# Linear attention's denominators as 32 rows per 512 tokens on four column tiles, with the reciprocals spread to the partitions by DMA

## The chip, the cores and the metric

One Trainium2 chip, one of its cores. The metric is the device time of one execution in microseconds (us). The kernel before takes 504.74 us (median of 4 runs, 504.45 to 505.67).

Names of engines: PE multiplies matrices, PEld loads its weights, DVE is the vector engine, ACT the scalar (activation) engine, POOL the general-purpose engine, SP the one that issues most DMAs. PSUM is the memory that PE writes (8 banks of 512 floats per partition).

## The reference

Two attention blocks over the same `x` (2048 tokens, width 1024, 32 heads of 32) are mixed by a gate per token. Block A is linear attention, block B a local dilated attention that this change does not touch.

```python
x = A_x
g = sigmoid((x * gate_w).sum(-1, keepdims=True))
# block A, linear attention
q, k, v = split(x @ wqkv)                      # 32 heads of 32
phi = lambda t: where(t > 0, t + 1, exp(t)) + 1e-6
pq, pk = phi(q), phi(k)
kv  = einsum("bhsd,bhse->bhde", pk, v)         # 32 x 32 per head
z   = einsum("bhsd->bhd", pk)                  # 32 per head
num = einsum("bhqd,bhde->bhqe", pq, kv)
den = einsum("bhqd,bhd->bhq", pq, z)[..., None] + 1e-6
a   = merge_heads(num / den) @ A_wo
# block B: 8 keys per query, 2 apart, softmax, then @ B_wo     (not touched)
return g * a + (1 - g) * b
```

## The kernel before

The program lists its operations, with an estimated cost for each, and a planner orders them once, when the kernel is built. After that each engine is given its own list, in a fixed order, and waits on semaphores where an operand is not there yet. For a DMA the planner assumes that it lands `lat` us after the previous one, plus 2 us.

```python
            fin = o.end
            if o.chan is not None:
                dma_free = max(dma_free, o.end) + o.lat
                fin = dma_free + 2.0
```

In the last third of the kernel ("stage 3") `phi(q)` is made per chunk `u` of 512 tokens and per group `j` of four heads (128 partitions). `num / den` is got by scaling `phi(q)` with `1/den` first; `kv` has been folded into the output weights. `zbd` is a block-diagonal 128x128 matrix per group which holds each `z` 32 times, so that one full matmul gives each denominator already repeated on the 32 partitions that need it.

```python
        def numer(u, j):
            ...                                    # 8 matmuls of 512 columns into a bank
            phi(bank, p_, preg, 8 * u + j)         # ACT Exp, two DVE operations
            def over():
                db = main.next()
                P.op("pe", lambda e: e.matmul(db.ap(), zbd[:, j, :], p_, start=True, stop=True), ...)
                R, _ = RAr.next()
                P.op("act", ... activation(R, db.ap(), ACT.Ln, bias=eps) ...)
                P.op("act", ... activation(R, R, ACT.Exp, scale=-1.0) ...)
                P.op("dve", ... tensor_tensor(dst, p_, R, ALU.mult) ...)
            after(6 if u == 0 else 2, over)

        for n, (u, j) in enumerate(nums):          # 32 numerator groups
            numer(u, j)
            slot(0)
            if n == 1:
                turn()
            if 3 <= n < 11:
                fold(n - 3, 0); fold(n - 3, 1)
            if n >= 17:
                a_out(*outs.pop(0))                # output groups of A: 8 matmuls each, 128 tokens x 512 columns
                slot(0)
        ...                                        # rest of a_out, then 16 final tiles with B's output
```

Of the kernel before, what the change touches and what calls it, by code (L numbers as in the profile page):

```python
# [6 lines left out]
ACT = mybir.ActivationFunctionType  # L7
ALU = mybir.AluOpType
# [7 lines left out]
DH = 32  # L16
# [1086 lines left out]
def build_kernel(nc, A_x, A_wqkv, A_wo, B_x, B_wqkv, B_wo, gate_w, out):  # L1103
# [10 lines left out]
    def SB(shape, dtype, name, at=None):  # L1114
        n = SZ[dtype]
        for d in shape[1:]:
            n *= d
        if at is None:
            at = base[0]
            base[0] += (n + 31) // 32 * 32  # L1120
        uid[0] += 1
        h = nc.alloc_sbuf_tensor_at("%s_%d" % (name, uid[0]), list(shape), dtype, offset=at)
        return Tile("S", h, at, list(shape), dtype)
# [32 lines left out]
    GT = [("M", 1, 2, None)]  # L1156
    gt_hbm = nc.dram_tensor("gt_hbm", [4, 512], F32)

    def hb(p0, p1, half):
# [19 lines left out]
    kvbd = SB([128, 8, 128], BF16, "kvbd")  # L1179
    zbd = SB([128, 8, 128], BF16, "zbd")  # L1180
    kva = SB([128, 8, 33], F32, "kva")
# [16 lines left out]
    kvT = SB([128, 8, 128], BF16, "kvT", at=vr.t[1].lo)  # L1198
    RAr = Ring([SB([128, 512], F32, "ra%d" % i, at=t.lo) for i, t in enumerate((Er.t[0], Er.t[1], Lr.t[0], vr.t[0]))])
    mxr = SB([1, 4, 128], F32, "mxr", at=vr.t[2].lo)  # L1200
# [7 lines left out]
    osb = Ring([SB([128, 1024], BF16, "o%d" % i) for i in range(2)])  # L1208
    pr = Ring([SB([128, 512], BF16, "p%d" % i) for i in range(4)])
    base[0] = max(base[0], top_)  # L1210
# [12 lines left out]
    def plan(seen):  # L1223
# [45 lines left out]
        C("pool", lambda e: e.memset(kvbd[:], 0.0), 0.9, [kvbd.all()])  # L1269
        C("pool", lambda e: e.memset(zbd[:], 0.0), 0.9, [zbd.all()])  # L1270

# [288 lines left out]
        for j in range(4):  # L1560
            sl = slice(32 * j, 32 * j + 32)
            P.op("dve", lambda e, sl=sl: e.tensor_copy(zbd[sl, :, sl], kva[sl, :, 32:33].to_broadcast([32, 8, 32])), dps(256), reads=[kva.all()], writes=[zbd.all()])
            P.op("dve", lambda e, sl=sl: e.tensor_copy(kvbd[sl, :, sl], kva[sl, :, 0:32]), 0.3, reads=[kva.all()], writes=[kvbd.all()])
# [23 lines left out]
        def numer(u, j):  # L1587
            bank = main.next()
            w, wr = w_cols(2, j)
            xs, xr = x_chunk(u)  # L1590
            group(bank, w, xs, [wr, xr])
            tgt, c0 = pqn(u)
            dst, reg = tgt[:, j, c0:c0 + 512], tgt.part((j, j + 1), (c0, c0 + 512))
            if u == 0:
                p_, preg = dst, reg
            else:
                pt, _ = pr.next()
                p_, preg = pt[:, :], pt.all()
            phi(bank, p_, preg, 8 * u + j)
            def over():  # L1600
                db = main.next()
                P.op("pe", lambda e: e.matmul(db.ap(), zbd[:, j, :], p_, start=True, stop=True), mm(512), reads=[zbd.all(), preg], writes=[db.iv], name="den")  # L1602
                R, _ = RAr.next()
                P.op("act", lambda e: e.activation(R[:, :], db.ap(), ACT.Ln, bias=eps[:, :]), act(512), reads=[db.iv, eps.all()], writes=[R.all()])  # L1604
                P.op("act", lambda e: e.activation(R[:, :], R[:, :], ACT.Exp, scale=-1.0), act(512), reads=[R.all()], writes=[R.all()])  # L1605
                P.op("dve", lambda e: e.tensor_tensor(dst, p_, R[:, :], ALU.mult), 0.65, reads=[preg, R.all()], writes=[reg])
            after(6 if u == 0 else 2, over)

# [19 lines left out]

        nums = [(u, j) for u in range(4) for j in range(8)]
        outs = [(t, jh) for t in range(NT) for jh in range(2)]  # L1630
        for n, (u, j) in enumerate(nums):
            numer(u, j)
            slot(0)
            if n == 1:
                turn()
            if 3 <= n < 11:
                fold(n - 3, 0)
                fold(n - 3, 1)
            if n >= 17:
                a_out(*outs.pop(0))  # L1640
                slot(0)
        while later:
            slot(0)
        P.op("dve", lambda e: e.tensor_reduce(mx4[:, 2:3], qe[:, :], AX.X, ALU.max), 0.2, reads=[qe.all()], writes=[mx4.part((2, 3))], prio=1e5)
        while outs:
            a_out(*outs.pop(0))


        P.op("dve", lambda e: e.tensor_scalar(mx4[:, 1:2], mx4[:, 1:2], -1.0, None, op0=ALU.mult), 0.1, reads=[mx4.part((1, 2))], writes=[mx4.part((1, 2))], prio=1e5)

        def mx_out(e):
            with nc.allow_non_contiguous_dma(reason="512 maxima"):
                return e.dma_start(mx_hbm.rearrange("i p -> p i"), mx4[:, :])
        P.op("sp", mx_out, 0.6, reads=[mx4.all()], writes=[MX], chan="mxo", lat=8.0, prio=1e5)
        P.op("sp", lambda e: e.dma_start(mxr[0:1, :, :], mx_hbm[None, :, :]), 0.1, reads=[MX], writes=[mxr.all()], chan="mxi", lat=2.0, prio=1e5)
        P.op("dve", lambda e: e.tensor_reduce(mx1[:, :], mxr[:, :, :], AX.X, ALU.max), dps(512), reads=[mxr.all()], writes=[mx1.all()], prio=1e5)
        small = [mx1.all()]
        P.op("dve", lambda e: e.tensor_scalar(mx1[:, 2:3], mx1[:, 2:3], 2.0, None, op0=ALU.max), 0.1, reads=small, writes=small, prio=1e5)
        for o, i0, i1 in ((ALU.max, 0, 1), (ALU.mult, 0, 0), (ALU.mult, 2, 3)):
            P.op("dve", lambda e, o=o, i0=i0, i1=i1: e.tensor_tensor(mx1[:, i0:i0 + 1], mx1[:, i0:i0 + 1], mx1[:, i1:i1 + 1], o), 0.1, reads=small, writes=small, prio=1e5)  # L1660
        P.op("dve", lambda e: e.tensor_scalar(mx1[:, 0:1], mx1[:, 0:1], 40.0 / DH, None, op0=ALU.is_le), 0.1, reads=small, writes=small, prio=1e5)
        P.op("dve", lambda e: e.tensor_scalar(mx1[:, 2:3], mx1[:, 2:3], 1e18 / (4 * DH), None, op0=ALU.is_le), 0.1, reads=small, writes=small, prio=1e5)
        flag_op = P.op("dve", lambda e: e.tensor_tensor(flag[:, :], mx1[:, 0:1], mx1[:, 2:3], ALU.mult), 0.1, reads=small, writes=[flag.all()], prio=1e5)


        for t in range(NT):
            tgt, c0 = a_loc(t)
# [3 lines left out]
            for f0, f1 in parts:  # L1671
# [13 lines left out]
                if t == NT - 1 or f1 == 1024:  # L1685
                    c = f0 if t == NT - 1 else 0
                    P.op("sp", lambda e, e_=e_, r=r, o_=o_, c=c, f1=f1: e.dma_start(out2[e_, r * 128:(r + 1) * 128, c:f1], o_[:, c:f1]), 0.5,
                         reads=[o_.part((c, f1))], chan="out%d_%d" % (os_, c), lat=1.0)

        C("act", lambda e: e.preload_act_table_set("natural_log_exp_and_others"), 1.3, [])  # L1690
# [64 lines left out]
```

## Time and profile before

| | before |
|---|---|
| time, median of 4 (range) | 504.74 us (504.45 to 505.67) |
| span of the profiled execution | 502.5 us |
| stage 3 (explained below), first to last matmul | 170.0 us |
| last matmul's start to the end of the span | 4.6 us |

From the profile's page: the busy time of each engine (us, share of the span, instructions), and the chain of work that ended last, by engine.

```profile
PE 488.5 (97%) x5190; PEld 232.6 (46%) x5257; DVE 264.6 (53%) x456; ACT 192.9 (38%) x335; POOL 6.6 (1%) x30
...
PE 95%; issue 2%; DMA 1%; ACT 1%; SPq 0%; DVE 0%
```

PE is the limit, and the chain confirms it: what happens elsewhere costs only where PE waits.

The windows view of the stretch that changes: length, then busy us (and instructions) of PE, PEld, DVE, ACT and POOL, the granted clock, the DMA engines' busy share, and GB/s.

```profile
342.00:362.00 20.00, 19.82 (x90) 8.73 (x91) 16.33 (x31) 18.07 (x41) 0.00 (x0) 1.00 0.00 1
362.00:382.00 20.00, 19.89 (x93) 9.09 (x93) 14.67 (x27) 12.33 (x26) 0.00 (x0) 1.00 0.00 1
382.00:402.00 20.00, 19.89 (x93) 9.02 (x94) 12.21 (x22) 10.98 (x24) 0.00 (x0) 1.00 0.00 1
```

PE has next to no gaps, and the DMA engines are all but idle. The waits of PE there, 322 to 445 us (engine, waited for: us in total, times, longest):

```profile
PE ps_all L1324 <- issue: 0.2, 1, 0.2
```

The groups that the change replaces (busy us, mean ns of one, idle before it and why):

```profile
L1602 PE MATMUL ps_all<-p,zbd 128*128 128x512 bf16 x24 | 8.9, 380 | 0.0
L1602 PE MATMUL ps_all<-pq,zbd 128*128 128x512 bf16 x8 | 3.0, 379 | 0.0
L1604 ACT ACTIVATE ra<-ps_all,eps 128x512 f32<-128x512 f32 x32 | 21.5, 688 | 2.2 <-PE ps_all L1602 2.0
L1605 ACT ACTIVATE ra<-ra 128x512 f32<-128x512 f32 x32 | 19.9, 639 | 0.5
```

A matmul's 379 ns is its latency; one starts every 0.216 us. So the 32 denominators cost 32 x 0.216 = 6.9 us of PE. The DMA issue table (count, KB each, us from issue to landing): the first line below, a store of four rows, has no landing time, because the trace has 5 semaphore updates from DMA for it, where all others but one have 16.

```profile
gt_hbm<-gts SPq DMA_DIRECT2D x1, 8.0 KB
gt<-gt_hbm SPq DMA_DIRECT2D x1, 8.0 KB, 4.8
```

### The profile page before, as it was taken

The numbers are of one execution on the slowest core, as the hardware profiler recorded it, in microseconds if no ns is written. First come the engines' busy times: TensorE is split into PE (matmuls) and PEld (weight loads), VectorE is DVE, ScalarE is ACT, GpSimd is POOL, SyncE is SP. The second block draws the span as 40 slices with busy tenths as digits, with TensorE's granted clock in tenths as the row PEclk, the third lists the DMA queues.
The fourth block names the chain that finished last, engine by engine and source line by source line (L and its number), as shares of the span: only waits on it lengthen the run. The fifth ranks groups of instructions, "written<-read, shape, count | busy, mean of one in ns | idle before, by whom it ended". The sixth has DMA issues, their size and how long they took to land.

```text
span 502.5 us, 11582 instructions
## 1 busy us (share of the span) xinstructions
PE 488.5 (97%) x5190; PEld 232.6 (46%) x5257; DVE 264.6 (53%) x456; ACT 192.9 (38%) x335; POOL 6.6 (1%) x30
## 2 busy tenths in 40 slices
PE   8999999999999999999999999999999999999996
PEld 2444444444454444544544545444444444444443
DVE  3112235556667676454555464678776563234443
ACT  1111111111354454655554555479864543100000
POOL 5000000000000000000000000000000000000000
PEclk9999999999999999999999999999999999999999
DMA  8999990000024060100010100500000000011222
GB/s 222 207 204 314 353 270 1 1 0 1 12 86 139 22 198 27 34 23 23 23 39 21 33 1 3 170 0 1 0 2 0 2 0 1 1 43 64 83 78 73
DMA packets 47410, 34.92 MB, mean 69 GB/s; under 512 B 22261, under 2 KB 43125, under 8 KB 47354
## 3 DMA queue, kind: packets, MB, share of 16 engines
q1 hardware_dynamic: 46810, 33.59, 23.6%
q8 instruction: 43, 0.70, 0.6%
q10 hardware_dynamic: 544, 0.52, 0.4%
q14 instruction: 13, 0.11, 0.1%
HBM read 21.51 MB, written 8.40 MB: 60 GB/s over the span
## 4 chain that ended last, share of the span: by engine, by line
PE 95%; issue 2%; DMA 1%; ACT 1%; SPq 0%; DVE 0%
PE ps_all L1324 76%; PE ps_all L1677 11%; PE ps_all L1427 2%; PE ps_all L1447 2%; PE ps_all L1602 1%; PE ps_all L1452 1%; PE ps_all L1523 1%; DMA xT<-in_A_x_dram 1%; PE ps_all L1580 1%; ACT ra L1604 0%; PE ps_all L1392 0%; SPq L1294 0%; SPq L1299 0%; ACT e L1333 0%; ACT ra L1605 0%
## 5 line engine op out<-in xcount | busy, mean ns | idle before, releaser
L1324 PE MATMUL ps_all<-w,xT 128*128 128x512 bf16 x922 | 207.8, 379 | 5.6 <-issue 4.0
L1324 PE MATMUL ps_all<-xT,w 128*128 128x512 bf16 x747 | 169.2, 379 | 2.5 <-issue 1.9
L1324 PEld LDWEIGHTS ps_all<-w,xT 128*128 128x128 bf16 x960 | 91.3, 98 | 110.3 <-issue 1.7
L1324 PEld LDWEIGHTS ps_all<-xT,w 128*128 128x128 bf16 x768 | 73.9, 98 | 88.8 <-ACT ra L1604 0.6
L1677 PE MATMUL ps_all<-w,qT 128*128 128x512 bf16 (+1 forms) x259 | 55.2, 373 | 0.3
L1677 PEld LDWEIGHTS ps_all<-w,qT 128*128 128x128 bf16 x264 | 25.8, 98 | 29.7
L1335 DVE TENSOR_SCALAR e<-e 128x512 bf16<-128x512 bf16 x64 | 18.4, 291 | 38.9 <-ACT e L1331 25.3
L1355 DVE CAST vst<-ps_all 128x512 bf16<-128x512 f32 x15 | 10.4, 691 | 42.7 <-PE ps_all L1324 42.7
L1433 ACT ACTIVATE E<-ps_all 128x1824 bf16<-128x1824 f32 (+1 forms) x18 | 30.4, 1687 | 3.1 <-PE ps_all L1427 2.0
L1331 ACT ACTIVATE e<-ps_all 128x512 bf16<-128x512 f32 x32 | 19.1, 597 | 31.6 <-PE ps_all L1324 30.8
L1333 ACT ACTIVATE e<-ps_all 128x512 bf16<-128x512 f32 x32 | 19.2, 601 | 29.3 <-PE ps_all L1324 27.8
L1681 DVE SCALAR_TENSOR_TENSOR o<-ps_all,gm,xT 128x512 bf16<-128x512 f32 (+1 forms) x25 | 18.2, 729 | 23.0 <-PE ps_all L1677 22.8
L1280 DVE TENSOR_TENSOR mx<-mx,kT 128x1024 bf16<-128x1024 bf16 x32 | 20.7, 688 | 16.9 <-ACT kT L1356 16.8
L1280 DVE TENSOR_TENSOR mx<-mx,qT 128x1024 bf16<-128x1024 bf16 x32 | 20.7, 688 | 16.7 <-ACT qT L1359 16.6
L1356 ACT ACTIVATE vst<-ps_all 128x512 bf16<-128x512 f32 x17 | 10.1, 597 | 47.8 <-PE ps_all L1324 47.8
L1436 DVE TENSOR_TENSOR E<-E,msk 128x1824 bf16<-128x1824 bf16 (+1 forms) x18 | 19.8, 1100 | 14.5 <-ACT E L1433 14.5
L1462 DVE TENSOR_TENSOR qT<-ps_all,L 128x456 bf16<-128x456 f32 (+1 forms) x36 | 21.1, 624 | 7.7 <-ACT L L1461 7.7
L1359 ACT ACTIVATE qT<-ps_all 128x512 bf16<-128x512 f32 x15 | 9.0, 597 | 37.0 <-PE ps_all L1324 37.0
L1337 DVE SCALAR_TENSOR_TENSOR pk<-ps_all,e 128x512 bf16<-128x512 f32 x32 | 22.0, 688 | 0.8
L1604 ACT ACTIVATE ra<-ps_all,eps 128x512 f32<-128x512 f32 x32 | 21.5, 688 | 2.2 <-PE ps_all L1602 2.0
L1356 ACT ACTIVATE az<-ps_all 128x512 bf16<-128x512 f32 x19 | 11.4, 600 | 27.6 <-PE ps_all L1324 27.6
L1356 ACT ACTIVATE kT<-ps_all 128x512 bf16<-128x512 f32 x14 | 8.4, 597 | 35.5 <-PE ps_all L1324 35.5
(77 smaller groups left out, 336.5 us busy)
## 6 DMA issues: line engine op xcount, KB each, us to landing
w<-in_A_wqkv_dram SPq DMA_DIRECT2D x6, 1024.0 KB, 8.2
v<-vB_hbm SPq DMA_DIRECT2D x36, 128.0 KB, 2.6
vB_hbm<-vst SPq DMA_DIRECT2D x32, 128.0 KB, 4.9
w<-in_B_wqkv_dram SPq DMA_DIRECT2D x4, 1024.0 KB, 8.3
out_dram<-o SPq DMA_DIRECT2D x15, 256.0 KB, 2.0
w<-in_A_wo_dram SPq DMA_DIRECT2D x2, 1024.0 KB, 5.6
w<-in_B_wo_dram SPq DMA_DIRECT2D x2, 1024.0 KB, 6.5
w<-in_B_wqkv_dram SPq DMA_DIRECT2D x6, 256.0 KB, 4.1
```

What stands on the lines that cost most here:

```text
L1280: P.op("dve", lambda e, m=m, op=op: e.tensor_tensor(m[:, 0:n], m[:, 0:n], src, op), 0.08 + n / 1920.0, reads=[m.all(), reg], writes=[m.all()],
L1324: last = e.matmul(bank.ap(), lhs(dc), rhs(dc), start=(dc == 0), stop=(dc == 7))
L1331: P.op("act", lambda e: e.activation(e_[:, :], bank.ap(), ACT.Exp), act(512), reads=[bank.iv], writes=[e_.all()])
L1333: P.op("act", lambda e: e.activation(e_[:, :], bank.ap(), ACT.Exp, accum_out=qe[:, col:col + 1]), act(512) + 0.1, reads=[bank.iv], writes= ...
L1335: P.op("dve", lambda e: e.tensor_scalar(e_[:, :], e_[:, :], 1.0, 1e-6, op0=ALU.min, op1=ALU.add), 0.25, reads=[e_.all()], writes=[e_.all()])
L1337: P.op("dve", lambda e: e.scalar_tensor_tensor(out=dst, in0=bank.ap(), scalar=0.0, in1=e_[:, :], op0=ALU.max, op1=ALU.add), dps(512), read ...
L1356: fa = lambda e: e.activation(dst, src(), ACT.Copy)
L1433: P.op("act", lambda e: e.activation(E[:, 0:32 * nq].rearrange("p (j q) -> p j q", j=4), ps[:, 4:8, 0:8 * nq], ACT.Exp), act(32 * nq), rea ...
L1436: P.op("dve", lambda e: e.tensor_tensor(ev(), ev(), m[:, :, :].rearrange("p r q -> p (r q)")[:, None, :].to_broadcast([128, 16, 2 * nq]), ...
L1462: P.op("dve", lambda e, L=L, pb=pb, g=g: e.tensor_tensor(qT[:, 4 * g:4 * g + 4, t0 + qs:t0 + qs + 2 * nq].rearrange("p c (h q) -> p h c q" ...
L1604: P.op("act", lambda e: e.activation(R[:, :], db.ap(), ACT.Ln, bias=eps[:, :]), act(512), reads=[db.iv, eps.all()], writes=[R.all()])
L1677: last = e.matmul(bank.ap(0, f1 - f0), qT[:, dc, t * 128:(t + 1) * 128], ws[3][:, dc, f0:f1], start=(dc == 0), stop=(dc == 7))
```

## The change

The intent: stop spending a full 128-column matmul on each group of four heads only to repeat every denominator 32 times. With `zsel`, 32 columns per group, eight groups fit into one PSUM bank on four column tiles that work side by side: 8 narrow matmuls per chunk in place of 8 full ones, and one Ln and one Exp per chunk in place of eight. The repetition moves to DMA: the tile of reciprocals is written to DRAM and read back eight times, each read spreading four rows over 128 partitions. To give this way time, the output groups start three numerator groups later, and three output tiles are moved ahead of the last chunk's output groups.

```diff
-    zbd = SB([128, 8, 128], BF16, "zbd")
+    zsel = SB([128, 8, 32], BF16, "zsel")
+    rc_hbm = nc.dram_tensor("rc_hbm", [4, 128, 512], F32)
+    RBr = Ring([SB([128, 512], F32, "rb%d" % i, at=kT.lo + 2048 * i) for i in range(12)])
...
+        def over(u):
+            tgt, c0 = pqn(u)
+            db = main.next()
+            def fn(e):
+                for q in range(2):
+                    for c in range(4):
+                        last = e.matmul(db.ap()[32 * c:32 * c + 32, :], zsel[:, 2 * c + q, :], tgt[:, 2 * c + q, c0:c0 + 512], start=(q == 0), stop=(q == 1),
+                                        tile_position=(0, 32 * c), skip_group_check=True)
+                return last
+            P.op("pe", fn, 0.55, mode="c", ...)
+            ...                                   # ACT: Ln, then Exp(-x), on R [128, 512]
+            P.op("sp", lambda e: e.dma_start(rc_hbm[u, :, :], R[:, :]), 0.5, ..., lat=1.0)
+            for j in range(8):
+                B, bs = RBr.next()
+                r0 = 32 * (j // 2) + 4 * (j % 2)
+                src = rc_hbm[u, r0:r0 + 4, :][:, None, :].to_broadcast([4, 32, 512])
+                last_in[0] = P.op("sp", lambda e, B=B, src=src: e.dma_start(B[:, :], src), 0.5, ..., chan="rci%d" % bs, lat=1.2)
+                P.op("dve", lambda e, B=B, dst=dst: e.tensor_tensor(dst, dst, B[:, :], ALU.mult), 0.65, ...)
...
+            if j == 7:
+                after(3, lambda u=u: over(u))     # denominators of chunk u: three groups after its last numerators
-            if n >= 17:
+            if n >= 20:
                 a_out(*outs.pop(0))
...
+        EARLY = 3
+        for t in range(EARLY):
+            while len(outs) > 8:
+                a_out(*outs.pop(0))
+            final(t)
```

More of the change, by code (lines that the diff above doesn't have):

```diff
@@ L1198, in build_kernel @@
     kvT = SB([128, 8, 128], BF16, "kvT", at=vr.t[1].lo)
-    RAr = Ring([SB([128, 512], F32, "ra%d" % i, at=t.lo) for i, t in enumerate((Er.t[0], Er.t[1], Lr.t[0], vr.t[0]))])
+    RAr = Ring([SB([128, 512], F32, "ra%d" % i, at=t.lo) for i, t in enumerate((Er.t[0], Er.t[1]))])
+    RBr = Ring([SB([128, 512], F32, "rb%d" % i, at=kT.lo + 2048 * i) for i in range(12)])
     mxr = SB([1, 4, 128], F32, "mxr", at=vr.t[2].lo)
@@ L1208, in build_kernel @@
     osb = Ring([SB([128, 1024], BF16, "o%d" % i) for i in range(2)])
-    pr = Ring([SB([128, 512], BF16, "p%d" % i) for i in range(4)])
     base[0] = max(base[0], top_)
@@ L1269, in plan @@
         C("pool", lambda e: e.memset(kvbd[:], 0.0), 0.9, [kvbd.all()])
-        C("pool", lambda e: e.memset(zbd[:], 0.0), 0.9, [zbd.all()])
+        C("pool", lambda e: e.memset(zsel[:], 0.0), 0.3, [zsel.all()])
         C("dve", lambda e: e.memset(warm[:, :], 0.0), 0.15, [warm.all()])
@@ L1561, in plan @@
             sl = slice(32 * j, 32 * j + 32)
-            P.op("dve", lambda e, sl=sl: e.tensor_copy(zbd[sl, :, sl], kva[sl, :, 32:33].to_broadcast([32, 8, 32])), dps(256), reads=[kva.all()], writes=[zbd.all()])
+            for b in range(2):
+                P.op("dve", lambda e, sl=sl, b=b, c=4 * b + j: e.tensor_copy(zsel[sl, b:8:2, c:c + 1], kva[sl, b:8:2, 32:33]), 0.1, reads=[kva.all()], writes=[zsel.all()])
             P.op("dve", lambda e, sl=sl: e.tensor_copy(kvbd[sl, :, sl], kva[sl, :, 0:32]), 0.3, reads=[kva.all()], writes=[kvbd.all()])
@@ L1592, in numer @@
             tgt, c0 = pqn(u)
-            dst, reg = tgt[:, j, c0:c0 + 512], tgt.part((j, j + 1), (c0, c0 + 512))
-            if u == 0:
-                p_, preg = dst, reg
-            else:
-                pt, _ = pr.next()
-                p_, preg = pt[:, :], pt.all()
-            phi(bank, p_, preg, 8 * u + j)
-            def over():
-                db = main.next()
-                P.op("pe", lambda e: e.matmul(db.ap(), zbd[:, j, :], p_, start=True, stop=True), mm(512), reads=[zbd.all(), preg], writes=[db.iv], name="den")
-                R, _ = RAr.next()
-                P.op("act", lambda e: e.activation(R[:, :], db.ap(), ACT.Ln, bias=eps[:, :]), act(512), reads=[db.iv, eps.all()], writes=[R.all()])
-                P.op("act", lambda e: e.activation(R[:, :], R[:, :], ACT.Exp, scale=-1.0), act(512), reads=[R.all()], writes=[R.all()])
-                P.op("dve", lambda e: e.tensor_tensor(dst, p_, R[:, :], ALU.mult), 0.65, reads=[preg, R.all()], writes=[reg])
@@ L1607, in numer @@
-            after(6 if u == 0 else 2, over)
+            phi(bank, tgt[:, j, c0:c0 + 512], tgt.part((j, j + 1), (c0, c0 + 512)), 8 * u + j)
+        last_in = [None]
+        def over(u):
[7 more added lines that the diff above has]
+                return last
+            P.op("pe", fn, 0.55, mode="c", reads=[zsel.all(), tgt.part((0, 8), (c0, c0 + 512))], writes=[db.iv], name="den")
+            R, rs = RAr.next()
+            RC = [("R", u, u + 1, None)]
+            P.op("act", lambda e: e.activation(R[:, :], db.ap(), ACT.Ln, bias=eps[:, :]), act(512), reads=[db.iv, eps.all()], writes=[R.all()])
+            P.op("act", lambda e: e.activation(R[:, :], R[:, :], ACT.Exp, scale=-1.0), act(512), reads=[R.all()], writes=[R.all()])
+            P.op("sp", lambda e: e.dma_start(rc_hbm[u, :, :], R[:, :]), 0.5, reads=[R.all()], writes=[RC], chan="rco%d" % rs, lat=1.0)
+            for j in range(8):
+                B, bs = RBr.next()
+                r0 = 32 * (j // 2) + 4 * (j % 2)
+                src = rc_hbm[u, r0:r0 + 4, :][:, None, :].to_broadcast([4, 32, 512])
+                last_in[0] = P.op("sp", lambda e, B=B, src=src: e.dma_start(B[:, :], src), 0.5, reads=[RC], writes=[B.all()], chan="rci%d" % bs, lat=1.2)
+                dst, reg = tgt[:, j, c0:c0 + 512], tgt.part((j, j + 1), (c0, c0 + 512))
+                P.op("dve", lambda e, B=B, dst=dst: e.tensor_tensor(dst, dst, B[:, :], ALU.mult), 0.65, reads=[reg, B.all()], writes=[reg])
@@ L1627, in a_out @@
                 move(dst, src, 512, hold[h], reg, g[:, t:t + 1], [g.all()])
-        nums = [(u, j) for u in range(4) for j in range(8)]
-        outs = [(t, jh) for t in range(NT) for jh in range(2)]
-        for n, (u, j) in enumerate(nums):
-            numer(u, j)
-            slot(0)
-            if n == 1:
-                turn()
-            if 3 <= n < 11:
-                fold(n - 3, 0)
-                fold(n - 3, 1)
-            if n >= 17:
-                a_out(*outs.pop(0))
-                slot(0)
@@ L1642, in plan @@
-        while later:
-            slot(0)
-        P.op("dve", lambda e: e.tensor_reduce(mx4[:, 2:3], qe[:, :], AX.X, ALU.max), 0.2, reads=[qe.all()], writes=[mx4.part((2, 3))], prio=1e5)
-        while outs:
-            a_out(*outs.pop(0))
-        P.op("dve", lambda e: e.tensor_scalar(mx4[:, 1:2], mx4[:, 1:2], -1.0, None, op0=ALU.mult), 0.1, reads=[mx4.part((1, 2))], writes=[mx4.part((1, 2))], prio=1e5)
-        def mx_out(e):
-            with nc.allow_non_contiguous_dma(reason="512 maxima"):
-                return e.dma_start(mx_hbm.rearrange("i p -> p i"), mx4[:, :])
@@ L1654, in plan @@
-        P.op("sp", mx_out, 0.6, reads=[mx4.all()], writes=[MX], chan="mxo", lat=8.0, prio=1e5)
-        P.op("sp", lambda e: e.dma_start(mxr[0:1, :, :], mx_hbm[None, :, :]), 0.1, reads=[MX], writes=[mxr.all()], chan="mxi", lat=2.0, prio=1e5)
-        P.op("dve", lambda e: e.tensor_reduce(mx1[:, :], mxr[:, :, :], AX.X, ALU.max), dps(512), reads=[mxr.all()], writes=[mx1.all()], prio=1e5)
-        small = [mx1.all()]
-        P.op("dve", lambda e: e.tensor_scalar(mx1[:, 2:3], mx1[:, 2:3], 2.0, None, op0=ALU.max), 0.1, reads=small, writes=small, prio=1e5)
@@ L1659, in plan @@
-        for o, i0, i1 in ((ALU.max, 0, 1), (ALU.mult, 0, 0), (ALU.mult, 2, 3)):
-            P.op("dve", lambda e, o=o, i0=i0, i1=i1: e.tensor_tensor(mx1[:, i0:i0 + 1], mx1[:, i0:i0 + 1], mx1[:, i1:i1 + 1], o), 0.1, reads=small, writes=small, prio=1e5)
-        P.op("dve", lambda e: e.tensor_scalar(mx1[:, 0:1], mx1[:, 0:1], 40.0 / DH, None, op0=ALU.is_le), 0.1, reads=small, writes=small, prio=1e5)
-        P.op("dve", lambda e: e.tensor_scalar(mx1[:, 2:3], mx1[:, 2:3], 1e18 / (4 * DH), None, op0=ALU.is_le), 0.1, reads=small, writes=small, prio=1e5)
@@ L1663, in plan, with final @@
-        flag_op = P.op("dve", lambda e: e.tensor_tensor(flag[:, :], mx1[:, 0:1], mx1[:, 2:3], ALU.mult), 0.1, reads=small, writes=[flag.all()], prio=1e5)
-        for t in range(NT):
+        def final(t):
             tgt, c0 = a_loc(t)
@@ L1688, in plan @@
                          reads=[o_.part((c, f1))], chan="out%d_%d" % (os_, c), lat=1.0)
+        nums = [(u, j) for u in range(4) for j in range(8)]
+        outs = [(t, jh) for t in range(NT) for jh in range(2)]
+        for n, (u, j) in enumerate(nums):
+            numer(u, j)
+            if j == 7:
+                after(3, lambda u=u: over(u))
+            slot(0)
+            if n == 1:
+                turn()
+            if 3 <= n < 11:
+                fold(n - 3, 0)
+                fold(n - 3, 1)
+            if n >= 20:
+                a_out(*outs.pop(0))
+                slot(0)
@@ new lines, in plan @@
+        while later:
+            slot(0)
+        P.op("dve", lambda e: e.tensor_reduce(mx4[:, 2:3], qe[:, :], AX.X, ALU.max), 0.2, reads=[qe.all()], writes=[mx4.part((2, 3))], prio=1e5)
+        EARLY = 3
+        for t in range(EARLY):
+            while len(outs) > 8:
+                a_out(*outs.pop(0))
+            final(t)
+        while outs:
+            a_out(*outs.pop(0))
+        P.op("dve", lambda e: e.tensor_scalar(mx4[:, 1:2], mx4[:, 1:2], -1.0, None, op0=ALU.mult), 0.1, reads=[mx4.part((1, 2))], writes=[mx4.part((1, 2))], prio=1e5)
@@ new lines, in mx_out @@
+        def mx_out(e):
+            with nc.allow_non_contiguous_dma(reason="512 maxima"):
+                return e.dma_start(mx_hbm.rearrange("i p -> p i"), mx4[:, :])
+        P.op("sp", mx_out, 0.6, reads=[mx4.all()], writes=[MX], chan="mxo", lat=8.0, prio=1e5, after=[last_in[0]])
+        P.op("sp", lambda e: e.dma_start(mxr[0:1, :, :], mx_hbm[None, :, :]), 0.1, reads=[MX], writes=[mxr.all()], chan="mxi", lat=2.0, prio=1e5)
+        P.op("dve", lambda e: e.tensor_reduce(mx1[:, :], mxr[:, :, :], AX.X, ALU.max), dps(512), reads=[mxr.all()], writes=[mx1.all()], prio=1e5)
@@ new lines, in plan @@
+        small = [mx1.all()]
+        P.op("dve", lambda e: e.tensor_scalar(mx1[:, 2:3], mx1[:, 2:3], 2.0, None, op0=ALU.max), 0.1, reads=small, writes=small, prio=1e5)
+        for o, i0, i1 in ((ALU.max, 0, 1), (ALU.mult, 0, 0), (ALU.mult, 2, 3)):
+            P.op("dve", lambda e, o=o, i0=i0, i1=i1: e.tensor_tensor(mx1[:, i0:i0 + 1], mx1[:, i0:i0 + 1], mx1[:, i1:i1 + 1], o), 0.1, reads=small, writes=small, prio=1e5)
+        P.op("dve", lambda e: e.tensor_scalar(mx1[:, 0:1], mx1[:, 0:1], 40.0 / DH, None, op0=ALU.is_le), 0.1, reads=small, writes=small, prio=1e5)
@@ L1690, in plan @@
+        P.op("dve", lambda e: e.tensor_scalar(mx1[:, 2:3], mx1[:, 2:3], 1e18 / (4 * DH), None, op0=ALU.is_le), 0.1, reads=small, writes=small, prio=1e5)
+        flag_op = P.op("dve", lambda e: e.tensor_tensor(flag[:, :], mx1[:, 0:1], mx1[:, 2:3], ALU.mult), 0.1, reads=small, writes=[flag.all()], prio=1e5)
+        for t in range(EARLY, NT):
+            final(t)
         C("act", lambda e: e.preload_act_table_set("natural_log_exp_and_others"), 1.3, [])
```

## The prediction

> # Prediction
>
> **What bounds the kernel.** PE. The page's busy table: PE 488.5 of 502.5 us (97%), DVE 53%, ACT 38%. The chain of waits is 95% PE. In the stretch that changes (322 to 443 us, windows view) PE is busy 19.8 to 19.9 of every 20 us; the waits of PE there sum to 0.2 us. A 512-column matmul costs 0.216 us of PE (10.79 us per 50 in the chain). DMA is idle from 330 to 440 us.
>
> **Removed.** 32 full-array denominator matmuls: 32 x 0.216 = 6.9 us of PE, all on the chain. Also 28 of 32 Ln and Exp pairs (0.69 + 0.64 us), 37 us of ACT, off the chain.
>
> **Added on PE.** Four groups of 8 matmuls on 4 column tiles. The gate has this shape: 32 matmuls in 1.84 us, so four run together, 0.23 us a round. Two rounds plus the mode change (issue gaps of 0.16 us beside the score groups; the Trainium skill, TensorEngine Tiling (Array Packing), Key Properties, says a mode change drains the engine) is about 0.55 us, 2.2 us in all. PE gains 4.5 to 5 us: 500 us if nothing waits.
>
> **Added on DMA, and why I doubt 500.** Per 512 tokens, one 256 KB write and eight 256 KB broadcast reads whose source has an outermost size of 4. The Trainium skill, DMA: Bandwidth & Descriptors, "Why a DMA increments its semaphore by 16 and not by 1", says the engines used are the largest number up to 16 that divides both outermost sizes: 4 here. This trace agrees for the 4-row gate store: 5 semaphore updates came from DMA where others have 16, and the issue table has no landing time for it. A 2 KB packet took a median 84 to 87 ns, so a chunk's 1024 packets over 4 engines take about 21.5 us (estimate); over 16, 5.4 us. The kernel's planner assumes 9.6 us.
>
> Denominator to last scaled tile (estimate): 0.5 PE, 1.35 Ln and Exp, 2.5 write, 2 first read, 21.5 reads, 0.7 multiply, 1 of semaphores: 29.5 us. Between the first chunk's denominators and the first output group reading it, PE has 11 numerator groups (1.73 each), 4 folds, one denominator group: 20.4 us. PE waits about 9 us there. For later chunks enough PE work lies between (31 us for the last, with the 3 moved tiles), but DVE runs in an order planned for earlier landings: its multiplies come 8 to 10 us late and hold PSUM evacuations behind them. Eight banks cover some 8 us, so about 3 us more over three chunks.
>
> **Sum.** 504.9 - 4.7 + 9 + 3 = 512; the moved tiles look tuned on a chip, so I shade it to 510. Range 499.5 to 518. Faster by over 2%: 2%; within: 78%; slower: 20%.
>
> **What would show it.** PE busy falls to about 484 us. The reads have no landing time; DMA share is near a quarter for 20 us per chunk. PE waits for DVE's multiply 6 to 11 us once near 350 to 365 us; DVE waits for reads 2.7 us apart. If 16 engines serve the reads, the share is near 1 for 6 us, nothing waits, and the time is 500. The end is unchanged.
>
> **What would make it wrong.** Reads spread over 16 engines; packets faster than 84 ns; the planner putting other PE work before the first output group; deeper DVE blocking than eight banks cover, which costs 10 us more.

## The result

| | before | after |
|---|---|---|
| time, median of 4 (range) | 504.74 us (504.45 to 505.67) | 518.86 us (517.12 to 519.31) |
| ratio | | 1.0273 (95%: 1.0254 to 1.0292) |
| span of the profiled execution | 502.5 us | 517.6 us |
| stage 3, first to last matmul, same matmuls | 171.7 us | 182.9 us |
| last matmul's start to the end of the span | 4.6 us | 6.9 us |

The stage row is read from the trace: from the transposes of `turn()` to the last matmul. The kernel after has one numerator group more in that stretch (8 weight loads more), so 8 x 0.216 = 1.7 us are added to the 170.0 us of before.

The change makes the kernel 2.7% slower, just outside the range (499.5 to 518) that I gave. The same views of the kernel after, first the page: busy times, then two rows of 40 slices of the span (granted clock in tenths; DMA busy share in tenths), and the chain.

```profile
PE 498.6 (96%) x5257; PEld 231.6 (45%) x5257; DVE 258.2 (50%) x452; ACT 166.8 (32%) x287; POOL 6.0 (1%) x30
...
PEclk9999999999999999999999999999797999999999
DMA  8999980000042160100100004002222212221121
...
PE 83%; DMA 10%; SPq 3%; DVE 1%; ACT 1%; issue 0%
```

In what follows L1325 is a numerator group or an output group (8 matmuls of 512 columns), L1606 the denominators, L1336 and L1338 the two DVE steps of `phi`, L1621 the multiply by the reciprocals (before: L1324, L1602, L1335, L1337, L1606).

DMA is now on the chain, and there are two slices in which PE got less than its full clock. The windows, as before:

```profile
342.00:362.00 20.00, 18.16 (x90) 7.77 (x87) 10.79 (x22) 8.43 (x23) 0.00 (x0) 1.00 0.21 79
362.00:382.00 20.00, 17.25 (x74) 7.03 (x75) 10.97 (x20) 5.62 (x14) 0.00 (x0) 0.83 0.26 101
382.00:402.00 20.00, 14.80 (x62) 5.75 (x60) 9.53 (x19) 4.59 (x11) 0.00 (x0) 0.83 0.26 98
```

DVE and ACT do less than before, so neither is short of time; PE lost matmuls (62 in 20 us where it did 93). The DMA engines sit at a quarter of their capacity, 0.26 and about 100 GB/s, for as long as the reads last: 0.26 of 16 engines is 4.2 engines' worth, the flat level to be expected if each read runs on 4 (s16, below, tests that). The new groups, and the reads in the issue table, with no landing time:

```profile
L1606 PE MATMUL ps_all<-xT,zsel 128*32 128x512 bf16 x24 | 2.7, 542 | 9.2 <-DVE xT L1338 9.2
L1612 ACT ACTIVATE ra<-ps_all,eps 128x512 f32<-128x512 f32 x4 | 2.7, 686 | 9.9 <-PE ps_all L1606 9.9
L1613 ACT ACTIVATE ra<-ra 128x512 f32<-128x512 f32 x4 | 2.5, 632 | 0.1
```

```profile
rb<-rc_hbm SPq DMA_DIRECT2D x32, 256.0 KB
```

The waits of PE, and those of DVE for the reads:

```profile
PE ps_all L1606 <- DVE xT L1338: 9.2, 2, 5.2
...
PE ps_all L1325 <- DVE pq L1621: 0.6, 1, 0.6
PE ps_all L1325 <- DVE xT L1359: 0.4, 1, 0.4
```

```profile
DVE xT L1621 <- DMA rb<-rc_hbm: 29.8, 20, 1.9
...
DVE pq L1621 <- DMA rb<-rc_hbm: 9.7, 7, 1.9
```

So PE's long waits are not where I had put them (L1325 waiting for the multiply L1621: only 0.6 us) but before the denominators of the second and the third chunk (L1606), and what they wait for is no multiply: L1338 is the last step of `phi`, which needs no reciprocal at all. The timeline of PE there (start, length, what, and the idle time before it):

```profile
364.14 1.05 PE L1606 MATMUL ps_all<-xT,zsel 128*32 128x512 bf16 x8 [3.98 <-DVE xT L1338]
365.12 5.53 PE L1325 MATMUL ps_all<-xT,w 128*128 128x512 bf16 x16
371.26 1.90 PE L1325 MATMUL ps_all<-w,pq 128*128 128x512 bf16 x8 [0.60 <-DVE pq L1621]
...
390.45 1.04 PE L1606 MATMUL ps_all<-xT,zsel 128*32 128x512 bf16 x8 [5.20 <-DVE xT L1338]
391.42 3.60 PE L1325 MATMUL ps_all<-w,pq 128*128 128x512 bf16 x8
```

and of DVE just before the first of these waits ended:

```profile
357.68 0.69 DVE L1621 TENSOR_TENSOR pq<-pq,rb 128x512 bf16<-128x512 bf16 x1 [0.95 <-DMA rb<-rc_hbm]
360.25 0.69 DVE L1621 TENSOR_TENSOR pq<-pq,rb 128x512 bf16<-128x512 bf16 x1 [1.88 <-DMA rb<-rc_hbm]
360.85 0.49 DVE L1336 TENSOR_SCALAR e<-e 128x512 bf16<-128x512 bf16 x2
362.80 0.69 DVE L1621 TENSOR_TENSOR pq<-pq,rb 128x512 bf16<-128x512 bf16 x1 [1.45 <-DMA rb<-rc_hbm]
363.40 0.68 DVE L1338 SCALAR_TENSOR_TENSOR xT<-ps_all,e 128x512 bf16<-128x512 f32 x1
```

Read it from below: `phi`'s last step (363.40) stands behind the multiply at 362.80 in DVE's fixed list, which waits for a read; the reads land 2.56 us apart. The multiply does not concern the second chunk, but DVE cannot pass it. PE, which needs that `phi` for the second chunk's denominators, idles until 364.14. And after each wait PE runs slow: 16 matmuls take 5.53 us, where they take 3.63 at full clock (junk, below). The trace's clock records show half clock from 362.18 to 369.01 and from 389.49 to 396.32, 6.83 us each.

### The profile page after: what moved, and what is told of

Same layout as the page of the kernel before. It is cut to its first block, busy times and chain, and to the rows that moved or that the text cites. A ratio compares the mean times of both kernels' runs of the same rounds, so it can differ in the third digit from the quotient of the medians. Undisturbed runs are those within 1.5% of the kernel's fastest.

```text
span 517.6 us, 11655 instructions
## 1 busy us (share of the span) xinstructions
PE 498.6 (96%) x5257; PEld 231.6 (45%) x5257; DVE 258.2 (50%) x452; ACT 166.8 (32%) x287; POOL 6.0 (1%) x30
## 4 chain that ended last, share of the span: by engine, by line
PE 83%; DMA 10%; SPq 3%; DVE 1%; ACT 1%; issue 0%
PE ps_all L1325 65%; PE ps_all L1654 11%; DMA rb<-rc_hbm 8%; SPq L1619 3%; PE ps_all L1428 2%; PE ps_all L1448 2%; DMA rc_hbm<-ra 2%; PE ps_all L1453 1%; DMA xT<-in_A_x_dram 1%; PE ps_all L1524 1%; PE ps_all L1606 1%; PE ps_all L1582 1%; ACT ra L1612 0%; DVE xT L1338 0%; PE ps_all L1393 0%; ACT ra L1613 0%
## 5 line engine op out<-in xcount | busy, mean ns | idle before, releaser
L1325 PE MATMUL ps_all<-w,xT 128*128 128x512 bf16 x960 | 215.7, 382 | 1.3 <-DMA xT<-in_A_x_dram 0.9
L1325 PE MATMUL ps_all<-xT,w 128*128 128x512 bf16 x768 | 174.3, 383 | 0.0
L1325 PEld LDWEIGHTS ps_all<-w,xT 128*128 128x128 bf16 x960 | 91.9, 98 | 112.1 <-issue 5.2
L1325 PEld LDWEIGHTS ps_all<-xT,w 128*128 128x128 bf16 x768 | 74.7, 99 | 91.4 <-issue 5.3
L1336 DVE TENSOR_SCALAR e<-e 128x512 bf16<-128x512 bf16 x64 | 18.4, 290 | 33.1 <-ACT e L1332 25.2
L1356 DVE CAST vst<-ps_all 128x512 bf16<-128x512 f32 x15 | 10.4, 693 | 46.1 <-PE ps_all L1325 46.1
L1621 DVE TENSOR_TENSOR xT<-xT,rb 128x512 bf16<-128x512 bf16 x24 | 16.5, 691 | 29.8 <-DMA rb<-rc_hbm 29.8
L1357 ACT ACTIVATE vst<-ps_all 128x512 bf16<-128x512 f32 x17 | 10.2, 598 | 49.4 <-PE ps_all L1325 49.4
L1338 DVE SCALAR_TENSOR_TENSOR pk<-ps_all,e 128x512 bf16<-128x512 f32 x32 | 22.1, 689 | 0.8
L1461 ACT ACTIVATE L<-ps_all 128x456 f32<-128x456 f32 (+1 forms) x36 | 17.8, 548 | 8.6 <-PE ps_all L1453 8.6
```

Source lines behind the costliest of these rows:

```text
L1325: last = e.matmul(bank.ap(), lhs(dc), rhs(dc), start=(dc == 0), stop=(dc == 7))
L1336: P.op("dve", lambda e: e.tensor_scalar(e_[:, :], e_[:, :], 1.0, 1e-6, op0=ALU.min, op1=ALU.add), 0.25, reads=[e_.all()], writes=[e_.all()])
L1338: P.op("dve", lambda e: e.scalar_tensor_tensor(out=dst, in0=bank.ap(), scalar=0.0, in1=e_[:, :], op0=ALU.max, op1=ALU.add), dps(512), read ...
L1357: fa = lambda e: e.activation(dst, src(), ACT.Copy)
```

## Experiments

Theory A: DVE's fixed order, planned for reads 1.2 us apart, puts multiplies that wait ahead of `phi` steps that PE needs. Theory B: the data are simply too late for the output groups that use them (what I had predicted for the first chunk). Both have one root if the reads run on 4 engines; a third theory is that PE's own new work costs more than I thought. All edits below are to the kernel after, unless said otherwise. In the table, "stage 3" and "end" are read from each trace as above (the stage holds the same matmuls in all but "junk", which has 42 more); "wait" is the sum of PE's longer idle times in it (over about 0.35 us), taken between starts of matmuls and less one matmul's 0.216 us. (s16e0 and s16pool ran on another chip than the other experiments; each is compared with before on its own chip.)

| run | time, median (us) | ratio to before (95%) | stage 3 | wait | end |
|---|---|---|---|---|---|
| before (medians) | 504.2 to 504.7 | | 171.7 | 0 | 4.6 |
| after | 518.86 | 1.0273 (1.0254 to 1.0292) | 182.9 | 10.9 | 6.9 |
| peonly (wrong result) | 499.80 | 0.9906 (0.9887 to 0.9925) | 167.0 | 0 | 4.6 |
| s16 | 502.56 | 0.9966 (0.9938 to 0.9994) | 167.1 | 0 | 7.2 |
| lat26 | 510.68 | 1.0124 (1.0102 to 1.0147) | 175.9 | 6.7 | 6.8 |
| outs24 | 526.02 | 1.0426 (1.0406 to 1.0446) | 189.1 | 18.9 | 7.1 |
| junk | 519.04 | 1.0296 (1.0272 to 1.0320) | 183.9 | 6.1 | 7.1 |
| pool | 511.12 | 1.0131 (1.0113 to 1.0149) | 175.9 | 7.4 | 7.1 |
| early0 | 528.65 | 1.0482 (1.0464 to 1.0501) | 192.9 | 20.0 | 7.3 |
| s16f | 499.83 | 0.9925 (0.9903 to 0.9947) | 168.0 | 1.0 | 4.3 |
| s16e0 | 506.71 | 1.0041 (1.0029 to 1.0053) | 173.3 | 4.6 | 4.6 |
| s16pool | 499.87 | 0.9915 (0.9901 to 0.9928) | 167.0 | 0 | 4.4 |

The results of all but "peonly" agree with the reference.

### peonly: PE's part of the change alone

```diff
-            P.op("sp", lambda e: e.dma_start(rc_hbm[u, :, :], R[:, :]), ...)
-            for j in range(8):
-                ...                               # reads and multiplies
```

> The change without the write to DRAM, the broadcast reads and the multiplies (a wrong result on purpose): only the tensor engine's part of the change is left, with Ln and Exp of the four denominator tiles. If the loss comes from the way back of the reciprocals, this is 32 x 0.216 = 6.9 us less and 4 x 0.55 = 2.2 us more than before: 499.5 to 501 us, no wait of PE over 1 us and no stretch at half clock between 20 us and the end. If the column tiles themselves, their mode changes or the 3 moved tiles cost the time, it is at 510 or more.

Measured: 499.80 us, stage 3 at 167.0 us, 4.7 us under before, no wait and no half clock after the start. So the column tiles do what was hoped: PE's sum in the prediction (4.7 us) was right, the third theory falls, and all of the loss comes from the way back.

### s16: the same reads on 16 engines

The eight reads of a chunk are cut differently: one per head of the group of four and per half of the groups, with 32 partitions as the outermost size on both sides. The bytes and the number of DMAs stay. (`zsel`'s columns are placed 16 apart in place of 4 so that a head's rows are evenly spaced. Two things come with it: a multiply now waits for four reads, and the reads also wait until the old contents of their buffers, `kT`, are done with.)

```diff
-    RBr = Ring([SB([128, 512], F32, "rb%d" % i, at=kT.lo + 2048 * i) for i in range(12)])
+    RBr = Ring([SB([128, 4, 512], F32, "rb%d" % i, at=kT.lo + 8192 * i) for i in range(3)])
-                src = rc_hbm[u, r0:r0 + 4, :][:, None, :].to_broadcast([4, 32, 512])
-                ... e.dma_start(B[:, :], src), ... lat=1.2)
+                    src = rc_hbm[u, :, :].rearrange("(j x) s -> x j s", x=16)[h, 4 * half:4 * half + 4, :][None, :, :].to_broadcast([32, 4, 512])
+                    ... e.dma_start(B[32 * h:32 * h + 32, :, :], src), ... lat=0.8)
```

> Same bytes and the same count of 8 reads of 256 KB per 512 tokens, but each read fills 32 partitions with 4 tiles' rows of one head, so that its outermost size is 32 on both sides. If the 4-engine reads are the root, 16 engines serve them: DMA share near 0.9 for about 6 us per chunk in place of 0.26 for 20 us, PE waits under 1.5 us in all, no half clock, 500 to 503 us. If the latency of the way through DRAM or the order on DVE is the root whatever the rate, PE still waits over 6 us and it stays at 511 or more.

Measured: 502.56 us; PE waits for nothing in stage 3, which takes 167.1 us, as with no way back at all. The reads in the issue table and the windows of the first chunk's reads:

```profile
rb<-rc_hbm SPq DMA_DIRECT2D x32, 256.0 KB, 6.7
```

```profile
347.00:352.00 5.00, 5.00 (x25) 2.27 (x24) 2.93 (x6) 1.95 (x6) 0.00 (x0) 1.00 0.99 222
352.00:357.00 5.00, 5.00 (x25) 2.25 (x23) 3.89 (x8) 1.89 (x7) 0.00 (x0) 1.00 0.88 182
```

Now there is a landing time, and the share is near 1 for about 10 us in place of 0.26 for 21 us (I had expected 6 us: a 2 KB packet took a median 149 ns here, where it took 84 in the kernel after; why is open). The trace counts 48 semaphore updates from DMA for three reads on one semaphore; in the kernel after it counts 15, five for each read: one early and then four close together (the first read of its semaphore: 348.47, then 352.00 to 352.51). That is the rule of the Trainium skill (DMA: Bandwidth & Descriptors, "Why a DMA increments its semaphore by 16 and not by 1"), as the prediction used it: an outermost size of 4 gives 4 engines. One reserve: with this cut the planner also put the second chunk's denominators two numerator groups later, so that DVE's own waits for reads (10.3 us here against 39.5) had more cover. The rest of the 2.8 us to peonly is the end, 7.2 us against 4.6; see s16f.

### lat26: the planner told the truth about the reads

```diff
-... chan="rci%d" % bs, lat=1.2)
+... chan="rci%d" % bs, lat=2.57)
```

> One number: the planner is told 2.57 us per read in place of 1.2. The reads stay on 4 engines. Theory A (DVE's fixed order puts the multiplies ahead of work that PE needs): DVE no longer stands in front of reads, PE waits under 2 us, no half clock, 500 to 504 us, though the reads still land 2.57 us apart. Theory B (the data are simply too late for the output groups, as my prediction had it for the first chunk): PE waits for the multiplies 6 us or more and it is 509 or more.

Measured: 510.68 us. The reads are as slow as before, but the planner now puts 15 numerator groups (in place of 11) between the first denominators and the first output group and spreads the multiplies. By the numbers set beforehand this is theory B's outcome (509 us or more, waits of 6 us or more). Both waits before denominators are gone, as theory A has it, and 8 us came back; but PE still waits 1.7 us for the first chunk's multiply and 4.7 us for one of the third chunk's, with 6.83 us of half clock around the longer:

```profile
PE ps_all L1325 <- DVE xT L1621: 4.7, 1, 4.7
PE ps_all L1325 <- DVE pq L1621: 1.7, 1, 1.7
```

So neither theory alone is right, and a better plan does not cover the slow reads. The new plan changes the order on DVE and the time given to the data at once, so this run cannot say how much each costs; pool, below, can.

### outs24: output groups start later still

```diff
-            if n >= 20:
+            if n >= 24:
```

> Output groups start after the 24th numerator group in place of the 20th, which gives the first chunk's data 7 us more; nothing else changes. Theory B (the first output group waits for its data, 9 us in my prediction): the loss goes, 503 to 508 us. Theory A (DVE's order holds the next chunk's denominators): PE still waits 4 us before the second chunk's denominators and some us before the third's, with half clock after, 513 to 519 us.

Measured: 526.02 us, worse than either theory said. Theory B's remedy does not help here: PE waits 3.6 us before the second chunk's denominators as it did before (theory A's mark), 1.0 before the third's and 9.1 before the fourth's, and 4.0 us in between for evacuations (L1359, on DVE too) of output groups. Theory A's kind of wait, then, but I had foreseen neither the fourth chunk's nor the total.

```profile
PE ps_all L1606 <- DVE xT L1338: 13.8, 3, 9.1
```

### pool: the multiplies taken off DVE

```diff
-                P.op("dve", lambda e, B=B, dst=dst: e.tensor_tensor(dst, dst, B[:, :], ALU.mult), 0.65, ...)
+                P.op("pool", lambda e, B=B, dst=dst: e.tensor_tensor(dst, dst, B[:, :], ALU.mult), 1.3, ...)
```

> The changed kernel with its 32 multiplies on POOL, which does nothing else there; reads still on 4 engines. Theory A (DVE's fixed order held the denominators): the two waits before the second and third chunk's denominators go. Theory B (data too late) then shows by itself: PE reaches the first output group about 363.7 us and its data come about 372 us, so one wait of about 8 us and 2 to 3 us at half clock, as I predicted for the change: 511 to 515 us. If it is 505 or less, lateness alone cost nothing and the order on DVE was all of it; if the waits before the denominators stay, theory A falls.

Measured: 511.12 us, in the range given. POOL takes 1.16 us for a multiply and stands waiting for reads, which hurts nobody. The waits of PE in the whole execution (but for those at its start):

```profile
PE ps_all L1325 <- POOL pq L1621: 7.2, 1, 7.2
```

This is the prediction's one wait, at 362.7 to 370.1 us, where the first output group needs the first chunk's data. So the two causes come apart: with the reads slow, lateness alone makes stage 3 175.9 - 167.0 = 8.9 us longer than peonly's, and having the multiplies in DVE's list adds 182.9 - 175.9 = 7.0 us. PE's own order is nearly the same in both: 11 numerator groups stand between the first denominators and the first output group, and the second chunk's denominators come one group earlier in pool, which leaves less time for the `phi` they need, not more.

### junk: PE kept busy where it waited

```diff
+            def junk(e):
+                for _ in range({1: 18, 2: 24}[u]):
+                    last = e.matmul(db.ap(), warm[:, 0:128], warm[:, :], start=True, stop=True)
+                return last
+            if u in (1, 2):
+                P.op("pe", junk, 0.0, reads=[warm.all()], writes=[db.iv], name="junk")
             P.op("pe", fn, 0.55, mode="c", ...)   # the denominators
```

> The changed kernel, with 18 and 24 needless matmuls (zeros, 0.216 us each, so 3.9 and 5.2 us) put on PE just where it waited 4.0 and 5.2 us for DVE. If PE's idling is what brings the half clock of 6.83 us that follows each of the two waits, the needless work costs nothing and saves the 5.4 us lost at half clock: 512 to 515 us, and no clock record below 1.0 between 20 us and the end. If the half clock has another cause, it stays and the time is 518 to 522 us.

Measured: 519.04 us, the same as after, and no saving. The timeline of PE:

```profile
356.88 4.05 PE L1611 MATMUL ps_all<-warm 128*128 128x512 bf16 x18
360.76 1.89 PE L1325 MATMUL ps_all<-xT,w 128*128 128x512 bf16 x8
362.62 0.62 PE L1606 MATMUL ps_all<-xT,zsel 128*32 128x512 bf16 x8
363.17 3.63 PE L1325 MATMUL ps_all<-xT,w 128*128 128x512 bf16 x16
369.72 2.39 PE L1325 MATMUL ps_all<-w,pq 128*128 128x512 bf16 x8 [2.93 <-DVE pq L1627]
...
419.97 1.90 PE L1325 MATMUL ps_all<-w,xT 128*128 128x512 bf16 x8 [2.84 <-DVE xT L1359]
```

My expectation was half right. The half clock at these two places is gone (denominators in 0.62 us in place of 1.05, the 16 matmuls after them in 3.63 in place of 5.53), so idling did bring it. But the 2 us won at once turn into a wait of 2.93 us for the multiply at the next output group, with a new record at half clock (3.41 us) around its end. Counted from the first matmul of stage 3, this output group starts at 43.3 us here and at 43.4 in the kernel after: the reads set the pace, and PE at half clock had only been filling time in which the next data were not there. The later wait of 2.84 us is for an evacuation that stands in DVE's list behind a multiply waiting for its read. (The second filler was somewhat too long: the third chunk's denominators start 1.7 us after their `phi` is ready, so "no saving" holds to about 1.5 us, against the 5.4 hoped for.) The half clock is real and was almost free in this kernel. Subtracting it as a loss of its own would count the same microseconds twice.

### early0: the three output tiles not moved up

```diff
-        EARLY = 3
+        EARLY = 0
```

> The changed kernel with the 3 output tiles not moved up. The last chunk's last multiply ended at 449.5 us, and PE would reach the last chunk's output groups at 441.9: a wait of about 7.6 us and 2 to 3 us at half clock, 527 to 531 us. If the moved tiles cover nothing, the time stays at 517 to 520 us.

Measured: 528.65 us, as expected. PE waits 7.7 us at the last chunk's first output group and runs at half clock a third time after it:

```profile
PE ps_all L1325 <- DVE xT L1621: 7.7, 1, 7.7
```

The moved tiles are cover for the last chunk, and without them the change would cost 4.8%.

### s16f: the end

In the kernel after, SP waits at the very end for the semaphores of every DMA channel, 14 more than before. The DMAs of the way through DRAM are already waited for by the multiplies, so this version leaves those 14 out; otherwise it is s16.

```diff
-        self.final = [(self.csem[c], n) for c, n in chan_n.items()]
+        self.final = [(self.csem[c], n) for c, n in chan_n.items() if not c.startswith(("rci", "rco"))]
```

> The 16-engine version, whose end does not wait again for the 14 semaphores of the way through DRAM (their DMAs are waited for by the multiplies already). The stretch after the last matmul took 7.15 us in it and 6.9 in the changed kernel, 4.56 before. If the added waits at the end lengthen it, it comes back to about 4.6 us and the time to 499.5 to 501 us, 1% under before; if something else does (the fetch of the instructions after the branch), it stays near 7 us and the time at 502 to 503 us.

Measured: 499.83 us (two of its six runs took 502.2, the others at most 499.9; why is open); the end takes 4.3 us. The two groups of traces do not mix: with the 14 waits 6.8 to 7.3 us (7 kernels), without 4.3 to 4.6 us (5 kernels). So the 14 waits lengthen the end by about 2.5 us. How they do is open: they are 7 instructions of SP, 0.06 us apart, 0.4 us in all (whether it is the waiting or only seven instructions more before the branch was not tested), and in the kernel after most of the time lay after them, from SP's branch (514.5) to its next instruction (517.3), which took 0.5 us before.

### s16e0 and s16pool: is the rest of the tuning still needed, and is there more?

```diff
# s16e0: s16f with
-            if n >= 20:
+            if n >= 17:
-        EARLY = 3
+        EARLY = 0
# s16pool: s16f with
-                    P.op("dve", ... tensor_tensor(dst, dst, B[:, i, :], ALU.mult), 0.65, ...)
+                    P.op("pool", ... tensor_tensor(dst, dst, B[:, i, :], ALU.mult), 1.3, ...)
```

> The 16-engine version without the other tuning of the change: output groups start after the 17th numerator group again, and no output tile is moved up (the end as in s16f). If both only covered the slow reads, they are worth nothing now: 499 to 501 us, no wait of PE over 1.5 us. If they do something of their own, PE waits over 2 us before a first output group of a chunk and it is at 503 us or more.

Measured: 506.71 us; I was wrong. PE waits 4.0 us for a multiply of the last chunk, and 3.4 us of half clock follow (from 430.27 us):

```profile
PE ps_all L1325 <- DVE xT L1626: 4.0, 1, 4.0
```

Between the last chunk's denominators (410.4 us) and its own output groups PE now has only 8 output groups (13.8 us), where s16f has 11 and the three moved tiles (19.0 + 10.4 us), and even on 16 engines the way through DRAM took 18 to 19 us. The cover that the change adds is of use with fast reads too; which of its two parts would have been enough was not run.

> The 16-engine version (end as in s16f) with the multiplies on POOL. PE's own part of the change alone took 499.8 us, so no more than the 0.9 us that s16f waited before one denominator group is to be had: 498.5 to 500.5 us. If POOL's multiplies (1.16 us each against 0.69) come too late or hinder DVE, PE waits over 2 us and it is at 502 us or more.

Measured: 499.87 us, no wait in stage 3. It is as fast as s16f and as peonly, which has no way back at all: with 16 engines there is nothing more to get from this side. s16f and s16pool, 0.9% under before, beat both kernels, though not by the 2% that would count as clearly faster.

## Why the prediction was wrong

**Right: PE's gain.** 4.7 us predicted, 4.7 us measured in stage 3 of peonly. (A group of eight narrow matmuls took 0.64 us of PE rather than the 0.55 forecast, 0.4 us more in all; where that came back was not traced. The gap of 0.16 us that the prediction saw after the score groups is one of the holes of the trace of before: the first matmul after the group is missing there, and the trace of after has it 0.14 us after the group's last start.)

**Right: the 4 engines, their rate and the delay.** 2.7 us between reads predicted, 2.56 measured; five semaphore updates per read; share 0.26. From the first chunk's denominators (343.04) to the end of its last multiply (371.19) it took 28.2 us; I had said 29.5.

**Right in place, once alone: the wait at the first output group.** About 9 us predicted; with the multiplies off DVE it is 7.2 us of wait, and 8.9 us of stage 3 with the slow clock that follows. That the sum comes so near to 9 is luck: the wait was some 2 us shorter than forecast, and a clock that was not in the forecast made up for it. In the kernel after it is hidden behind an earlier wait, and only 0.6 us is left to see there.

**Wrong: DVE's part, "Eight banks cover some 8 us, so about 3 us more over three chunks".** This is the step that failed. It measured 7.0 us (after against pool). I asked how many PSUM banks PE could fill before it stalls, but another consumer comes first: the next chunk's denominators. The second chunk's stand three numerator groups (5.2 us) after its last numerators, the third's only an output group and a numerator group (3.5 us), and the `phi` between stood behind multiplies in DVE's list: PE waited 4.0 and 5.2 us there. The bound was the tightest consumer of the blocked engine, not the buffer with the most room. The prediction did name deeper blocking on DVE as what would make it wrong, at 10 us more, but left no room for that at the top of its range.

**Wrong: "The end is unchanged".** 14 further semaphores to wait for made it 2.3 us longer in the profile; without those waits it goes back.

**Not in the sum: the clock.** After its longer waits PE ran at half clock for 3.4 or 6.8 us (10.2 in outs24). The Trainium skill (TensorE: Matmul & The Clock Gate, Part 1: The HAM clock gate) says that PE falls to half rate after an idle window of about 3.4 us and comes back after as long a busy one; the traces agree only in part. Records at half clock are 3.4, 6.8 or 10.2 us long, and each of PE's waits of about 4 us or more had one. But of the waits between 2.8 and 3.7 us two had one (2.9 and 3.0) and two had none (2.8 and 3.6), so the length of a wait does not decide. What fits every case is a fixed grid: from its beginning to its last matmul, each trace has its changes of clock whole multiples of 3.41 us apart. In the 11 stretches of this grid at whose end the clock fell, PE had been idle for 2.11 us (s16e0) to 3.41; in those at full clock at whose end it did not fall, for at most 2.04 (s16e0, the stretch before). The 2.9 us of junk put 2.15 into one stretch; the 3.6 us of outs24 were split into 1.93 and 1.87. (Idle time is counted from 0.216 us after the last matmul's start; the few hundredths between 2.04 and 2.11 should not be leant on.) I knew that page and left the term out. It cost 1.5 us in pool, and next to nothing more in the kernel after, as junk showed.

The sum with the measured terms: 504.7 - 4.7 + 8.9 + 7.0 + 2.3 = 518.2 us, against 518.9 measured. This is bookkeeping, not a test: 8.9 and 7.0 are differences of the same traces and add up to after minus peonly whatever their causes. (In the profiled pair 1.6 us more lie at the very start, where the kernel after got its full clock at 10.6 us and the kernel before at 5.7; outs24, which starts with the same instructions as the others, shows it too, and pool and lat26 do not, so I take it for chance, which was not tested.) My own sum was 512, and shading it to 510 because the moved tiles "look tuned on a chip" went the wrong way: they do cover the last chunk, but only that one.

**PE busy** did not fall to 484 us but rose to 498.6: the trace of before lacks 67 matmuls (67 holes of 0.05 or 0.16 us, 7.5 us in all, which the trace of after does not have), and matmuls at half clock count for up to twice as long. In peonly it is 491.6, in pool 492.6. Busy time of PE was a poor thing to bet on.

## What to carry to other kernels

The outermost size of a broadcast read decided how many engines served it: with 4 it took twice as long as with 32 on both sides (the only two sizes run here). A missing landing time and a flat DMA share of a quarter were the signs. When engines run fixed lists, an operation that waits for a slow transfer delays everything behind it in its list: give it to an engine with nothing urgent to do, or plan it with the transfer's measured time, and ask which consumer of the blocked engine comes first. Before adding up waits and slow-clock losses, test whether removing one only lengthens the next.

## What the Trainium skill lacked or had wrong

- DMA: Bandwidth & Descriptors: its rule for the number of engines held (5 semaphore updates from DMA per read with an outermost size of 4, 16 with 32). Its measured rates have no read that runs on few engines and no broadcast: on 4 engines a read of 256 KB landed every 2.56 us at a share of 0.26, about 102 GB/s; on 16, the same broadcast bytes moved at 182 to 222 GB/s at a share of 0.88 to 0.99, so the rate rose by about two, not four, as a 2 KB packet took 149 ns in place of 84.
- TensorE: Matmul & The Clock Gate: an idle window of about 3.4 us, as Part 1 has it, was more than was needed: the clock fell at the end of stretches of 3.41 us in which PE had been idle for 2.11 us or more, and did not at 2.04 or less. What the page lacks is a warning that the loss need not add to the time: keeping PE busy removed the half clock at both places and left the time at 519.0 against 518.9 us.
- TensorEngine Tiling (Array Packing): it gives no time for a change of tiling mode. Here a group of 8 matmuls on four column tiles took 0.55 us from its first start to the next full matmul's, and about 0.1 us more before it.
- No page that I read has a price for further semaphores to wait for at the end of a program: 14 more went with 2.3 to 2.9 us more after the last matmul, of which their own instructions are 0.4.
